# An attention, a dense block and eight experts in one program: a branch laid out the other way, a weight conversion spread over three steps, matmuls regrouped, and one store made conditional

## The chip, the cores and the metric

The kernel runs on one core of a Trainium2 chip. That core has a matrix engine (TensorE, PE in the profile; its weight loads are listed apart as PEld), VectorE (DVE), ScalarE (ACT), GpSimd (POOL) and SyncE (SP). Each engine takes its own list of instructions in order and waits on semaphores for the others. The metric is device time in microseconds (us) of the whole program, smaller being better.

## The reference, cut to what matters

```python
# q, k, v: 2 batches x 8 heads x 768 tokens x 64; a query sees the keys of its own 6-bit bucket
scores = np.where(q_bucket[..., :, None] == k_bucket[..., None, :], q @ k.T / 8, -1e9)
x = (softmax(scores) @ v)                       # as 1536 tokens x 512
h = x @ w_in                                    # 512 -> 2048, weights given as 64-bit floats
g = np.where(h >= 1, h, np.where(h <= -1, 0, (h + 1) ** 2 / 4))
x = g @ w_out                                   # 2048 -> 512
# gate: two experts of 8 for each token, with weights top2_w
for e in range(8):
    for k in range(2):
        mask = top2[:, k] == e
        out[mask] += top2_w[mask, k, None] * (np.maximum(x[mask] @ w1[e], 0) @ w2[e])
```

Which experts a token goes to is known only on the chip, so the size of each expert's work is data.

## The kernel before, in words

The order of all work is written out by hand. There are three stages in a row, with the gate between the last two.

**Attention** (class `Attention`, `run`). There are 96 steps, one for each 128 queries of a head, and four more to drain. Step `t` issues on TensorE the scores of step `t` (L178, L180), the transposes of the probabilities of step `t - 4` (L209), and, from `t = 10` on, one call of `values` (L217): the product of one block of 128 transposed keys with the values of two heads. Six calls fill one PSUM bank. Every sixth step TensorE also computes the bucket bits of a new head (L158). VectorE takes the row minimum of the scores (L189) and some small columns (L191 to L195), ScalarE the exponential (L197) and the copies of the transposes out of PSUM (L210), GpSimd the division by the row sum (L200). The scores have two PSUM buffers: scores `t + 2` wait for the exponential of `t`.

**Dense block** (class `Dense`). 64 pairs (token block c of 384, feature block f of 128) are walked in order. Step `i` issues `hidden` for pair `i` (12 matmuls, L561, into bank `i % 2`) and then `out` for pair `i - 2` (9 matmuls, L584, into three banks). All matrices are split into a high and a low part so that three products make one exact one. `hidden` goes on with ScalarE (L567), VectorE (L570, L573), ScalarE (L574, the high part `gh`) and GpSimd (L575, the low part `gl`). The weights come as 64-bit floats and have to be converted on the chip, one feature block of 1024 columns at a time, in eight steps (`Weights.steps`): an absolute value on ScalarE (L315), a clip (L316) and a shift (L317) on VectorE, four bit combinations of half a block each on VectorE (L311), and a split into high and low part on ScalarE and GpSimd (L307, L308). The first three blocks are converted during the attention, the other 13 in the dense block, one every second step from step 2 on. Before the change all but the split are issued in one step, between the instructions of `hidden`, and the split in the next.

**Experts** (class `Experts`). Nine jobs `j`: the first takes tokens of expert 0 from the first nine token tiles, the second the rest of expert 0, the others one expert each. A job works on a block `o = 0` of up to 384 tokens and, where more came, on further blocks `o = 1, 2, 3`. A block has 11 steps: L720 computes hidden features of step `i`, L714 multiplies those of step `i - 3` by the second matrix; ScalarE and VectorE split the hidden features (L747, L748). Each step exists in up to four widths, chosen by a branch on TensorE alone (L729, L731, L739) from the count of tokens. ScalarE and VectorE also split the weights of the next job (L931, L932). Tokens are gathered by GpSimd (L682), turned by TensorE (L699), and results are scaled by VectorE (L752) and added to the output by GpSimd's scatters (`scatter`, L688, with a small memset L687 ahead of each).

Between two jobs stands `further` (L797): a branch on all five engines that asks whether the job has further blocks. Its one side runs block `o` (11 steps in all widths, and the next `further` inside it); its other side, `over`, stores the rows of the last block, between which stand the first three steps of the next job. Before the change the second side is laid out right behind the branch, and from its end TensorE must jump over the whole first side. The count `more` is read into registers (L843) just ahead of the branch. In the profiled data jobs 0 and 2 have a further block, and the others have none. After job 8 `over` stores all three blocks of 128 rows, whatever the count.

Of the kernel before, what the change touches and what calls it, by code (L numbers as in the profile page):

```python
# [41 lines left out]
NG = TOK // HT  # L42
# [26 lines left out]
class Attention:  # L69
# [175 lines left out]
    def run(self, hooks, drain):  # L245

        lag, nt, plan = 4, self.nt, {}
        for a in range(2):
            for i, j in enumerate((1, 1, 2, 3 + 4 * a, 3, 4)):
                plan.setdefault(j + 4 * a, []).append((self.prep, a, i))  # L250
            plan.setdefault(5 + 6 * a, []).append((self.proj, a, f"x{a}"))
        self.start()
        done = 0
        for t in range(nt + 4):
            pr, j = divmod(t, 12)
            if t < nt:
                self.scores(t)
            if t >= lag:
                self.transposes(t - lag)
            self.soft(t)  # L260
            self.flush(2 if j < 2 else 1)
            if pr < 7:
                for f, a, i in plan.get(j, []):
                    f(2 * pr + 2 + a, i)
            if pr < 8 and j == 0:
                self.load_v(pr)
            if pr < 6 and j in (6, 11):
                self.load(2 * pr + 4 + (j == 11))
            for f in hooks.get(t, []):
                f()  # L270
            if t >= lag + 6:
                self.values(*divmod(t - lag - 6, 6))
                done += 1
            if t >= nt:
                drain(t - nt)
        while done < nt:
            self.values(*divmod(done, 6))
            done += 1
        self.flush()
# [263 lines left out]
class Dense:  # L543
# [8 lines left out]
    def py(self, c):  # L552
        return self.banks[5:8] if c == 1 else self.banks[2:5]

    def hidden(self, i, c, f, extra):
        nc, p, w = self.nc, self.banks[i % 2][:, :HT], self.wt.W[f]
        V, A = nc.vector, nc.scalar
        n = 0
        for k in range(4):
            for a, x in ((0, 0), (0, 1), (1, 0)):  # L560
                nc.tensor.matmul(p, w[:, a, cols(k, 128)], self.X[c][:, x, k], start=n == 0, stop=n == 11)  # L561
                n += 1
        a = self.sb.tile([128, HT], F32, name="ga", bufs=2)
        gh = self.sb.tile([128, HT], F32R, name="gh", bufs=3)
        gl = self.sb.tile([128, HT], F32R, name="gl", bufs=3)
        self.G[c, f] = gh, gl
        A.activation(a, p, AF.Relu, bias=self.half[:, 0:1], scale=0.5)  # L567
        for e in extra[:2]:
            e()
        V.scalar_tensor_tensor(a, a, 1.0, a, op0=ALU.min, op1=ALU.mult)  # L570
        for e in extra[2:3]:
            e()
        V.tensor_tensor(a, p, a, op=ALU.max)  # L573
        A.activation(gh, a, AF.Copy)  # L574
        nc.gpsimd.tensor_sub(gl, a, gh.bitcast(F32))  # L575
        for e in extra[3:]:
            e()

    def out(self, c, f):
        gh, gl = self.G.pop((c, f))  # L580
        w = self.wt.W[f]
        for t in range(3):
            for i, (g, a) in enumerate(((gh, 0), (gh, 1), (gl, 0))):
                self.nc.tensor.matmul(self.py(c)[t], g[:, cols(t, 128)], w[:, a, 512:1024],  # L584
                                      start=f == 0 and i == 0, stop=f == NF - 1 and i == 2)

    def run(self, convert, late, rows):
# [18 lines left out]
        def at(i, f):  # L606
            plan.setdefault(i, []).append(f)

        split = {}
        for i in range(4 * NF + lag):  # L610
            if i < 4 * NF:
                extra = []
                for j in [j for j, s in convert.items() if s == i]:
                    st = wt.steps(j)
                    extra += st[:-1]
                    split.setdefault(i + 1, []).append(st[-1])
                extra += split.get(i, [])
                self.hidden(i, *order[i], extra)
            if i >= lag:
                c, f = order[i - lag]  # L620
                self.out(c, f)
# [16 lines left out]
class Experts:  # L638
# [137 lines left out]
    def over(self, j, o, c):  # L776

        rows = self.rows(j, o)
        if j == NE:
            for f in rows:  # L780
                f()
            return
        if j == 0 and o == 0:
            for i in range(8 + LAG):
                self.tokens(1, 0, i, self.xr)
        for i in range(LAG):
            if i < len(rows):
                rows[i]()
            self.step(j + 1, 0, i, c)
            if j >= 1:  # L790
                self.prefetch(8 * self.expert(j + 1) + 4 + i)

    def further(self, j, o, more, c):

        if self.blocks(j, o) < 1:
            return self.over(j, o - 1, c)
        with self.tc.If(more > o - 1, preferred_fallthrough_block=False) as g:  # L797
            for f in self.rows(j, o - 1):
                f()
            if o > 1:  # L800
# [18 lines left out]
    def job(self, j, c, hooks={}):  # L819

        cn = self.first if j == 0 else self.cn[:, j - 1]
        for i in range(0 if j == 0 else LAG, 8 + LAG):
            self.step(j, 0, i, c)
            if j >= 2 and i == LAG:
# [9 lines left out]
                self.tokens(j + 1, 0, i, self.xr)  # L834
            if j and i == 5:
                self.gather(j, 1, self.xm)
        c = self.load(j + 1, 0) if j < NE else None
        self.further(j, 1, self.number(cn[:, NG:], NG - 1), c)
        return c

    def number(self, cn, most, engines=None):
# [185 lines left out]
```

## Time and profile before

| | us |
|---|---|
| median of 3 runs | 961.88 |
| lowest and highest | 960.09, 964.64 |
| the profiled execution | 965.52 |
| its span, from the first to the last instruction | 963.7 |
| TensorE busy in it | 875.0 |
| VectorE, ScalarE, GpSimd busy | 579.7, 433.1, 393.8 |
| mean granted clock of TensorE | 0.966 |

One execution is profiled; all start times below count from the first instruction of its span. A busy time is the time in which at least one instruction of that engine ran. "Idle before" names the engine or the queue whose signal ended the idle time; "issue" there means that the engine waited for nothing that the profile shows, so that its own list of instructions had not yet delivered one. TensorE's matmuls overlap, so the times of neighbouring rows overlap too. A granted clock of 1 is 2.4 GHz, one of 0.5 is 1.2 GHz.

### The profile page before, as it was taken

Reading aid. Unit: us, or ns where it says so; the run is one execution under the profiler, and the core shown is the slowest. Engines: PE = TensorE matmul, PEld = TensorE weight load, DVE = VectorE, ACT = ScalarE, POOL = GpSimd, SP = SyncE. Lnnn points to the kernel's source line nnn. Section 1 sums busy time; section 2 is a strip of 40 time slices with the busy share of each in tenths; the row PEclk is TensorE's granted clock in tenths of the full one; section 3 lists DMA queues with packets and bytes.
Section 4 is the critical chain, followed back from the end, with each engine's and each line's share of the span. In section 5 each row is a group of like instructions: output and inputs, shape, how many; then the busy total and the mean of one; then the engine's idle time right before and its main releaser. Section 6 shows DMA issues by size and latency. Waiting matters only on the chain.

```text
span 963.7 us, 13751 instructions
## 1 busy us (share of the span) xinstructions
PE 875.0 (91%) x4846; PEld 716.0 (74%) x4846; DVE 579.7 (60%) x1215; ACT 433.1 (45%) x786; POOL 393.8 (41%) x403
## 2 busy tenths in 40 slices
PE   5999999999999898999999999978988968989873
PEld 3666666666687777899899888867877857878763
DVE  7899999988378787532926725326333445354352
ACT  4787787788534434333334432214322334334240
POOL 7777776784244545322221320332123143140332
PEclk8999999999999999999999999979999979999987
DMA  4439212112560000000501421346535376483742
GB/s 148 157 107 265 83 50 83 50 50 94 201 274 1 1 0 1 1 1 1 198 1 63 145 69 36 70 81 159 165 79 134 124 213 167 164 223 101 202 91 37
DMA packets 39883, 98.49 MB, mean 102 GB/s; under 512 B 6080, under 2 KB 15296, under 8 KB 37696
## 3 DMA queue, kind: packets, MB, share of 16 engines
q1 hardware_dynamic: 30688, 73.69, 22.8%
q0 software_dynamic: 8912, 22.50, 11.2%
q8 instruction: 94, 1.54, 0.7%
q14 instruction: 45, 0.37, 0.1%
q10 hardware_dynamic: 144, 0.39, 0.1%
HBM read 80.00 MB, written 16.58 MB: 100 GB/s over the span
## 4 chain that ended last, share of the span: by engine, by line
PE 40%; DMA 33%; DVE 15%; ACT 5%; issue 3%; another core or an unknown queue 2%; POOL 1%; POOLq 0%; SPq 0%; ACTq 0%; DVEq 0%
DMA xr<-xd,idx 16%; DMA out_dram<-yT,il 9%; DMA xm<-xd,idx 8%; PE b L561 7%; PE b L584 7%; PE bank_x L217 6%; PE bank_t L209 5%; PE s L178 4%; DVE TB L311 4%; PE s L180 3%; DVE ga L570 2%; DVE st L189 2%; PE b L714 2%; PE b L720 2%
## 5 line engine op out<-in xcount | busy, mean ns | idle before, releaser
L714 PE MATMUL b<-W,hT 128*128 128x512 f32 x648 | 176.9, 416 | 39.3 <-issue 34.6
L714 PEld LDWEIGHTS b<-W,hT 128*128 128x128 f32 x648 | 122.6, 198 | 65.7 <-issue 41.5
L688 POOL DMA_INDIRECT out_dram<-yT,il x33 | 52.4, 1589 | 258.9 <-DVE yT L752 256.4
L748 DVE SCALAR_TENSOR_TENSOR hT<-b,hT 128x384 fp32r<-128x384 f32 x88 | 49.0, 556 | 178.8 <-ACT hT L747 177.2
L747 ACT ACTIVATE hT<-b 128x384 fp32r<-128x384 f32 x88 | 43.3, 492 | 236.2 <-PE b L720 235.5
L561 PE MATMUL b<-X,W 128*128 128x384 f32 x768 | 147.3, 340 | 0.0
L575 POOL TENSOR_TENSOR gl<-ga,gh 128x384 fp32r<-128x384 f32 x64 | 75.2, 1177 | 165.2 <-ACT gh L574 126.5
L561 PEld LDWEIGHTS b<-X,W 128*128 128x128 f32 x768 | 135.0, 189 | 6.2 <-issue 1.8
L200 POOL TENSOR_SCALAR p<-p,st 128x768 f32<-128x768 f32 x96 | 98.1, 1022 | 63.1 <-DVE st L195 51.4
L584 PE MATMUL b<-W,gh 128*128 128x512 f32 x384 | 120.7, 395 | 0.0
L197 ACT ACTIVATE p<-s,st 128x768 f32<-128x768 f32 x96 | 95.5, 995 | 41.7 <-DVE st L195 34.6
L189 DVE TENSOR_REDUCE st<-s 128x1 f32<-128x768 f32 x96 | 91.7, 955 | 17.7 <-PE s L180 16.1
L720 PEld LDWEIGHTS b<-XT,W 128*128 128x128 f32 x576 | 88.9, 197 | 5.3 <-issue 1.8
L720 PE MATMUL b<-XT,W 128*128 128x256 f32 (+2 forms) x576 | 91.7, 314 | 1.2 <-issue 1.1
L570 DVE SCALAR_TENSOR_TENSOR ga<-ga 128x384 f32<-128x384 f32 x64 | 46.9, 733 | 74.8 <-ACT ga L567 74.8
L932 DVE TENSOR_TENSOR W<-stage,W 128x1024 fp32r<-128x1024 f32 x64 | 78.3, 1224 | 22.0 <-ACT W L931 22.0
L584 PE MATMUL b<-W,gl 128*128 128x512 f32 x192 | 77.6, 404 | 12.8 <-POOL gl L575 12.8
L210 ACT ACTIVATE pT<-bank_t 128x384 f32<-128x384 f32 x192 | 83.4, 488 | 8.9 <-PE bank_t L209 7.9
L217 PE MATMUL bank_x<-pT,vt 128*64 128x384 f32 x384 | 81.8, 510 | 0.4 <-DVE KM L165 0.3
L720 PE MATMUL b<-XA,W 128*128 128x384 f32 (+1 forms) x480 | 81.5, 323 | 0.0
L574 ACT ACTIVATE gh<-ga 128x384 fp32r<-128x384 f32 x64 | 33.6, 525 | 105.9 <-DVE ga L573 105.9
L209 PE MATMUL bank_t<-ident,p 128*128 128x128 f32 x576 | 79.4, 274 | 1.4 <-ACT pT L210 1.4
(171 smaller groups left out, 1303.3 us busy)
## 6 DMA issues: line engine op xcount, KB each, us to landing
stage<-in_w_dram SPq DMA_DIRECT2D x64, 512.0 KB, 4.4
R<-in_wio_dram SPq DMA_DIRECT2D x16, 1024.0 KB, 7.3
raw<-in_qk_dram SPq DMA_DIRECT2D x15, 768.0 KB, 4.3
out_dram<-z SPq DMA_DIRECT2D x15, 256.0 KB, 4.9
vt<-in_vv_dram SPq DMA_DIRECT2D x8, 384.0 KB, 4.8
xd<-TB SPq DMA_DIRECT2D x3, 780.0 KB, 3.7
xd<-z SPq DMA_DIRECT2D x3, 260.0 KB, 6.0
xd<-rows SPq DMA_DIRECT2D x1, 780.0 KB, 6.0
```

What stands on the lines that cost most here:

```text
L189: V.tensor_reduce(st[:, 0:1], s[:, :, :HT], axis=AX.XY, op=ALU.min)
L197: self.A.activation(p.rearrange("p (a b) -> p a b", a=2), s[:, :, :HT], AF.Exp, bias=st[:, 2:3], scale=st[:, 3:4], accum_out=st[:, 5:6])
L200: self.G.tensor_scalar(self.P[t - 1], self.P[t - 1], ps[:, 5:6], 1.0, op0=ALU.mult, op1=ALU.mult)
L209: self.T.transpose(b[:, cols(j, 128)], p[:, cols(3 * g + j, 128)], self.ident)
L210: self.A.activation(self.PT[u, s][:, cols(g, 3), cols(i, 128)], b[:, :HT].rearrange("p (j q) -> p j q", j=3), AF.Copy)
L217: self.T.matmul(xp[cols(s, 64), :HT], self.vt[pr][:, s, kt, :], self.PT[u, s][:, kt, :], start=kt == 0, stop=kt == 5)
L561: nc.tensor.matmul(p, w[:, a, cols(k, 128)], self.X[c][:, x, k], start=n == 0, stop=n == 11)
L575: nc.gpsimd.tensor_sub(gl, a, gh.bitcast(F32))
L584: self.nc.tensor.matmul(self.py(c)[t], g[:, cols(t, 128)], w[:, a, 512:1024], start=f == 0 and i == 0, stop=f == NF - 1 and i == 2)
L714: self.T.matmul(self.banks[2 + b], h[:, a, cols(b, 128)], w2[:, x, 512:1024], start=i == LAG and n == 0, stop=i == LAG + 7 and n == 2)
L720: self.T.matmul(p, w[:, a, cols(k, 128)], X[:, x, k, :N], start=n == 0, stop=n == 11)
L932: nc.vector.tensor_sub(w[:, 1], d, w[:, 0].bitcast(F32))
```

## The change

Four edits. In `run` of the attention `values` is called twice in every second step and not once in each. In `Dense` the eight parts of a block's conversion are placed by a table over the steps s - 1 to s + 2 (s being the step that took seven of them before) and at four places of `hidden`: ahead of L567, behind it, between L570 and L573, and at the end. `out` walks its nine matmuls by operand and then by bank, so that the three that read `gl` come last. In `Experts`, `over` reads the last job's class of size and stores only the first block where the count is at most 128. `further` lays its first side behind the branch, so that `over` is the far side and runs straight on into the next job; the branch gets a label for `o = 1`, and each job places on all five engines, behind its step 6, a hint that this branch will likely be taken. `more` is read at the start of the job.

```diff
@@ Attention.run @@
-            if t >= lag + 6:
-                self.values(*divmod(t - lag - 6, 6))
-                done += 1
+            if t >= lag + 6 and (t - lag) % 2:
+                for _ in range(2):
+                    self.values(*divmod(done, 6))
+                    done += 1
@@ Dense.hidden @@
-    def hidden(self, i, c, f, extra):
+    def hidden(self, i, c, f, early, amid, mid, late):
+        for e in early:
+            e()
         A.activation(a, p, AF.Relu, bias=self.half[:, 0:1], scale=0.5)
-        for e in extra[:2]:
+        for e in amid:
             e()
         V.scalar_tensor_tensor(a, a, 1.0, a, op0=ALU.min, op1=ALU.mult)
-        for e in extra[2:3]:
+        for e in mid:
             e()
         V.tensor_tensor(a, p, a, op=ALU.max)
         A.activation(gh, a, AF.Copy)
         nc.gpsimd.tensor_sub(gl, a, gh.bitcast(F32))
-        for e in extra[3:]:
+        for e in late:
             e()
@@ Dense.out @@
-        for t in range(3):
-            for i, (g, a) in enumerate(((gh, 0), (gh, 1), (gl, 0))):
+        for i, (g, a) in enumerate(((gh, 0), (gh, 1), (gl, 0))):
+            for t in range(3):
@@ Dense.run @@
-        split = {}
+        conv = {}
+        for j, s in convert.items():
+            for n, (d, place) in enumerate([(-1, 1), (0, 2), (1, 3), (2, 0), (2, 0), (2, 0), (2, 0), (2, 1)]):
+                conv.setdefault(s + d, ([], [], [], []))[place].append(lambda j=j, n=n: wt.steps(j)[n]())
-                extra = []
-                for j in [j for j, s in convert.items() if s == i]:
-                    st = wt.steps(j)
-                    extra += st[:-1]
-                    split.setdefault(i + 1, []).append(st[-1])
-                extra += split.get(i, [])
-                self.hidden(i, *order[i], extra)
+                self.hidden(i, *order[i], *conv.get(i, ([], [], [], [])))
@@ Experts.over @@
         if j == NE:
-            for f in rows:
-                f()
+            n = self.number(self.cn[:, j - 1, o:o + 1], len(CLASSES) - 1)
+            with self.tc.If(n > 0) as g:
+                for f in rows:
+                    f()
+            with g.Else():
+                rows[0]()
             return
@@ Experts.further @@
-        with self.tc.If(more > o - 1, preferred_fallthrough_block=False) as g:
+        kw = {"label": f"further{j}"} if o == 1 else {}
+        with self.tc.If(more > o - 1, preferred_fallthrough_block=True, **kw) as g:
@@ Experts.job @@
+        more = self.number(cn[:, NG:], NG - 1)
...
+            if i == 6:
+                self.tc.mark_branch_hint_location(f"further{j}", "LikelyTaken", engines=list(mybir.ALL_ENGINES))
         c = self.load(j + 1, 0) if j < NE else None
-        self.further(j, 1, self.number(cn[:, NG:], NG - 1), c)
+        self.further(j, 1, more, c)
```

## Rows read from the trace of the kernel before

**Rows 1.** Busy us (count) of PE, PEld, DVE, ACT, POOL by stretch; clock, DMA, GB/s.
```profile
160.70:190.30 29.60, 29.60 (x186) 18.72 (x184) 28.39 (x64) 23.27 (x50) 21.45 (x23) 1.00 0.20 67
264.00:392.00 128.00, 116.18 (x570) 101.28 (x569) 98.65 (x131) 52.74 (x80) 64.34 (x38) 1.00 0.14 56
611.00:948.00 337.00, 295.34 (x1592) 262.70 (x1591) 147.14 (x223) 106.37 (x160) 89.92 (x100) 0.93 0.53 139
```

**Rows 2.** Timeline of TensorE, attention: start, us, line, operation, count.
```profile
25.11 0.62 PE L178 MATMUL s<-KS,QH 128*128 128x384 f32 x2
26.58 0.61 PE L178 MATMUL s<-KS,QH 128*128 128x384 f32 x2
...
41.43 0.61 PE L178 MATMUL s<-KS,QH 128*128 128x384 f32 x2
43.77 0.61 PE L178 MATMUL s<-KS,QH 128*128 128x384 f32 x2
...
258.96 4.74 PE L217 MATMUL bank_x<-pT,vt 128*64 128x384 f32 x28
```

**Rows 3.** Waits of 264 to 392 us: total us, times, longest.
```profile
PE b L584 <- POOL gl L575: 11.8, 11, 1.1
```

**Rows 4.** Timeline of two steps of the conversion, VectorE and GpSimd.
```profile
295.84 1.05 DVE L316 TENSOR_SCALAR TB<-TB 128x1024 f32<-128x1024 f32 x1 [2.08 <-ACT TB L315]
296.81 1.34 DVE L570 SCALAR_TENSOR_TENSOR ga<-ga 128x384 f32<-128x384 f32 x1
298.08 0.68 DVE L317 TENSOR_SCALAR TB<-TB 128x1024 int32<-128x1024 int32 x1
298.68 0.54 DVE L573 TENSOR_TENSOR ga<-b,ga 128x384 f32<-128x384 f32 x1
299.15 3.30 DVE L311 SCALAR_TENSOR_TENSOR TB<-R,TB 128x512 int32<-128x512 int32 x4
302.37 0.54 DVE L570 SCALAR_TENSOR_TENSOR ga<-ga 128x384 f32<-128x384 f32 x1
...
293.93 2.41 POOL L308 TENSOR_TENSOR W<-TB,W 128x1024 fp32r<-128x1024 f32 x1 [2.38 <-ACT W L307]
296.30 1.44 POOL L575 TENSOR_TENSOR gl<-ga,gh 128x384 fp32r<-128x384 f32 x1
303.69 2.40 POOL L308 TENSOR_TENSOR W<-TB,W 128x1024 fp32r<-128x1024 f32 x1 [2.39 <-ACT W L307]
```

**Rows 5.** Branches by line and engine: count, ns minimum/median/maximum, first and last start.
```profile
L797 PEldq COMPARE_BRANCH  x20: 67/1840/5479, 600.2 to 949.2; - x20
...
L797 ACTq COMPARE_BRANCH  x20: 34/38/55, 601.5 to 947.4; - x20
L797 DVEq COMPARE_BRANCH  x20: 43/47/72, 602.2 to 948.9; - x20
...
L731 PEldq COMPARE_BRANCH  x80: 65/176/4332, 659.6 to 912.2; - x80
```

**Rows 6.** TensorE's waits, 760 to 948 us (jobs 3 to 8): total us, times, longest.
```profile
PE b L714 <- issue: 26.4, 6, 9.0
```

**Rows 7.** Timeline of TensorE where one job passes into the next.
```profile
671.56 3.50 PE L714 MATMUL b<-W,hT 128*128 128x512 f32 x9 [3.59 <-DVE W L932]
...
739.33 3.14 PE L714 MATMUL b<-W,hT 128*128 128x512 f32 x9 [2.57 <-issue]
...
815.26 3.85 PE L714 MATMUL b<-W,hT 128*128 128x512 f32 x9 [3.90 <-issue]
...
821.09 2.23 PE L714 MATMUL b<-W,hT 128*128 128x512 f32 x9
```

**Rows 8.** Timeline of the end: a step of job 8, first and last scatter.
```profile
940.26 0.86 PE L714 MATMUL b<-W,hT 128*128 128x512 f32 x3
...
949.94 1.62 POOL L688 DMA_INDIRECT out_dram<-yT,il  x1 [12.79 <-DVE yT L752]
...
954.36 1.59 POOL L688 DMA_INDIRECT out_dram<-yT,il  x1 [0.87 <-issue]
```

## Prediction, made before the changed kernel ran

> **What bounds it now.** I read the busy times by stretch first. TensorE is busy all the time in the attention (29.60 of 29.60 us for twelve steps), and less in the stretch with the conversions (116.18 of 128.00) and in the experts (295.34 of 337.00, at a mean granted clock of 0.93) [rows 1]. So TensorE's own list sets the pace everywhere; it can be shortened in the first stretch, and its holes filled in the other two. The timelines and waits then say who ends each hole. In the conversion stretch it is GpSimd's `gl` alone, 11.8 us in eleven waits [rows 3]. In the experts the holes lie where one job passes into the next and end by "issue": TensorE's own list had nothing to give [rows 6, 7]. The branch rows say why: the same branch L797 costs 67 ns where it falls through and up to 5479 ns where it jumps, on TensorE alone; on ScalarE and VectorE it never costs over 72 ns [rows 5].
>
> **Attention.** A step without `values` takes 26.58 - 25.11 = 1.47 us on TensorE, one with it 43.77 - 41.43 = 2.34; so a lone call costs 0.87. At the end seven calls run back to back in 4.74 us, 0.68 each [rows 2]. Two steps cost 4.68 now, and 1.47 + 2.34 + 0.68 = 4.49 with both calls together: 0.19 less, and 45 such pairs make 8.6. That is one end. The other is VectorE, which is busy 28.39 us of the 29.60 that twelve steps take [rows 1]; 1.2 are free there, against 6 x 0.19 = 1.1 that TensorE gives back, and it would have to run without a gap. Steps now come alternately early and late, and scores `t + 2` wait for the exponential of `t`, behind VectorE's minimum. A loss is not excluded if that wait opens. I take 6 us off, two thirds of the bound, since the heavy stretches will be VectorE's and the light ones TensorE's; the ends are 9 off and 2 on.
>
> **Conversion.** Two steps hold one block. From one L316 to the next of its kind is a loop: ScalarE's L315, then L316, L570, L317, L573, the four L311, L570 again; VectorE stands idle 2.08 us in each round, waiting for L315 [rows 4]. L308 recurs every 303.69 - 293.93 = 9.76 us [rows 4]. After the change L315 and L317 are done a step ahead of need, and the L311 stand where VectorE waited for TensorE; the 2.08 goes. What is late next is VectorE with GpSimd. L570 takes 0.54 alone and 1.34 with `gl` running beside it [rows 4]: it waits until GpSimd is through. VectorE's round is then 3.30 + 1.05 + 0.68 + 2 x 0.54 + 2 x 0.54 = 7.2, and between the first L573 and the second L570 the data must still pass through two of the three ScalarE instructions behind which the 2.08 arises (L574, L567 and L315, which is gone): about half of it, 1.0. That is 8.2, and one more clash of 0.8 with L308 (2.41) or `gl` makes 9.0. Without clashes the 11.8 us of waits [rows 3] go wholly; with two or three the round stays near 9.76 and nothing goes. At 9.0 it is 0.76 shorter, over eleven rounds 8 us. I take 7, since some rounds will clash twice; ends 0 and 12. The reordered `out`, which asks for `gl` after six matmuls and not two, helps only these same waits. A block's split is now issued one step later; its first reader stands two steps behind, so this hides until the round is late by as much.
>
> **The far branch.** Jobs 3 to 7 lose 26.4 us to "issue" in six waits [rows 6], job 1 loses 3.59 (the row names L932, but L797 held the queue until then) [rows 7]: 30 us at six passages. Each also lowers the clock: behind job 4's passage nine L714 take 3.85 us, where nine take 2.23 a little later [rows 7], 1.6 more; six times that is an estimate of 10. Total 40. After the change these jobs jump at the branch, hinted five steps ahead, and `over` runs on without a jump. The trace has no hinted branch. Bounds: 67 ns, the fall-through, and 5479 ns, the far jump [rows 5]. I take 0.2 us, near the 176 ns median of L731 [rows 5], the nearest row of jumps whose target is held. What remains is the code behind the target: L731 too has a jump of 4332 ns [rows 5], so a jump into code not yet there stalls again. Three L720 steps stand at the head of `over` to cover it. I leave 2 us per passage, the middle between nothing and job 4's 3.90 [rows 7], and so take 40 - 12 = 28 off. Jobs 0 and 2 go the other way: they fall through, but inside they jump far without a hint and jump once more over `over`. One added far jump costs about what job 2's lone one does now, 2.57 us [rows 7]; without half of it covered, 1.5 each, so 3 back. Net 25 off; ends 3 on (hint without effect) and 37 off. The nine hints on five engines and the earlier read of `more` lie beside TensorE's queue: nothing, and if that cover is gone some tenths of a us per job.
>
> The Trainium skill speaks against this part (Runtime: NRT & Kernel Launch, section Instruction fetch mechanics): it says that prefetch is purely sequential and that a taken branch out of the fetched window must first fetch its target. The trace agrees for the branches it has, 67 ns against 5479 [rows 5]; no run here shows a hint. By the page alone the term would be 3 on and not 25 off.
>
> **The last store.** The three last scatters start at 949.94 and 954.36, 4.42 us from the first to the third [rows 8]. Job 8's steps have three L714 each [rows 8], one row block and so the lowest class: its count is at most 128 and one scatter stays. The added read and branch come while GpSimd waits 12.79 us for VectorE [rows 8] and cost nothing; if that cover failed, some 0.4 us. I take 4.4 off, ends 3 and 5.
>
> **Sum.** 6 + 7 + 25 + 4.4 = 42.4. The profiled execution took 965.5, so 923.1; it lies 3.6 above the median of the runs, which makes 961.9 - 42.4 = 919.5.
>
> **Rivals.** (a) *The hint has no effect*, so the far stall only moves from the end of `over` to the branch. For it: a taken branch here always paid when far, and the page named above states it as a rule. Against it: nothing in the trace, which has no hint. Then 961.9 - 6 - 7 - 4.4 + 3 = 947.5. (b) *VectorE takes over* in the attention and in the conversion: its 28.39 of 29.60 [rows 1] and the clash of L570 [rows 4] speak for it, the 2.08 us of idle time against it. Then 961.9 - 25 - 4.4 = 932.5. (c) *Slower:* the hinted target displaces the code in use on ScalarE or VectorE, which have no far jump at L797 now [rows 5]. Place: between step 6 and the end of each job. Price: a far fetch, some 4.4 us in eight jobs, 35 us, while TensorE gets nothing: 947.5 + 35 = 982.5. It decides the sign from 14 / 8 = 1.8 us per job. Against it: those engines hold few instructions per job.
>
> **Numbers.** Forecast 0.52, (a) 0.25, (b) 0.17, (c) 0.05; 0.01 is left. The forecast's own range is 905 to 931 (terms at 9, 11, 32 and 5 off, and at 2, 2, 23 and 4 off). The range of 8 in 10 is 904 to 949: it takes in (b) and about half of (a). About 0.5%, 4.8 us, is what a measurement can tell from no change. Slower by more is (c), 0.05; within it lies the upper edge of (a), 0.06; faster has 0.89.
>
> **What would show it.** Right: L797 on TensorE has no row over 1 us at the end of jobs 1 and 3 to 7, and the "issue" waits of 760 to 948 us fall from 26.4 to about 10; L308 recurs every 9.0 us and `gl` ends hardly any wait of TensorE; pairs of attention steps take 4.5 to 4.6 us; one scatter after the last matmul. Wrong: a far L797 of 3 to 5 us now at the branch itself (a); scores waiting for the exponential, or L308 still every 9.7 us (b); gaps on ScalarE or VectorE behind step 6 (c).

## The result, and the profile after

The changed kernel takes 931.02 us (median of four runs, 928.71 to 932.29), the kernel before 961.82 beside it (four runs, 960.09 to 964.64): a ratio of 0.9674, 95% interval 0.9642 to 0.9707, or 31 us less. Run once more beside other kernels it stood at 0.9629 (0.9606 to 0.9651), 36 us less. I had forecast 919.5 with a range of 904 to 949: the sign and the range hold, and the gain is three quarters of the 42.4 I had summed. That is closer than the reasons were, and in part luck: of the four terms one was nothing, one was nearly twice as large, one was half as large, and the largest came about in another way than I said. These errors cancel in part.

The profiled execution took 928.71 us with a span of 926.9. Most lines have moved: L308 is L309 here, L311 is L312, L316 and L317 are L317 and L318, L567 is L570, L570 and L573 are L573 and L576, L575 is L578, L688 is L689, L714 is L715, L720 is L721, L729 and L731 are L730 and L732, L752 is L753, L797 is L803. I read it in the order of the prediction. First the busy times by stretch, with the columns of [rows 1]; the last stretch begins 37 us earlier here, so that it ends as long ahead of the program's end. The stage has become shorter, so the same 337 us hold 1726 of TensorE's instructions where they held 1592.

```profile
160.70:190.30 29.60, 28.55 (x185) 19.09 (x185) 27.70 (x64) 23.00 (x51) 21.52 (x23) 1.00 0.19 67
264.00:392.00 128.00, 127.93 (x634) 111.98 (x631) 101.46 (x137) 57.66 (x84) 64.84 (x42) 1.00 0.14 56
574.00:911.00 337.00, 311.23 (x1726) 276.75 (x1726) 159.10 (x267) 110.48 (x168) 98.87 (x106) 0.97 0.54 143
```

Beside [rows 1] the three stretches went three ways. In the attention TensorE *lost* its full list: 28.55 of 29.60, with nearly the same count of instructions (185, before 186), where it was busy throughout before. In the conversion it has no hole left (127.93 of 128.00, before 116.18). In the experts it is busy 15.9 us more of the 337, at a granted clock of 0.97 after 0.93.

**Attention.** TensorE's waits from 35 to 240 us: total us, times, longest. Before, the first two had 1.0 in two waits and 0.3 in one.

```profile
PE s L178 <- ACT p L197: 4.6, 10, 1.1
PE bank_x L158 <- DVE X L222: 3.5, 6, 0.6
```

The scores wait for the exponential, as the prediction named it for the case where VectorE takes over, and L158, the first matmul of the next head, waits for L222, VectorE's eviction of the `values` just finished. VectorE's timeline shows what stands in front of that L222:

```profile
170.22 0.96 DVE L143 SCALAR_TENSOR_TENSOR QM<-raw,QH 64x768 fp32r<-64x768 f32 x1
171.21 0.96 DVE L189 TENSOR_REDUCE st<-s 128x1 f32<-128x768 f32 x1
172.19 0.15 DVE L191 TENSOR_SCALAR st<-st 128x1 f32<-128x1 f32 x1
172.27 0.78 DVE L193 SCALAR_TENSOR_TENSOR st<-st 128x2 f32<-128x2 f32 x1
172.97 0.15 DVE L195 RECIPROCAL st<-st 128x1 f32<-128x1 f32 x1
173.05 0.53 DVE L222 TENSOR_TENSOR X<-bank_x,X 128x384 fp32r<-128x384 f32 x1
```

From 170.22 to 173.58 these six follow each other without a gap, and L158 starts at 173.64. From the first scores to the last it is 234.89 us now, 235.66 before; then the attention's last calls take 17.39 us between the first and the third step of the dense layers where they took 14.41. (Of these 3.0 us, 1.7 belong to one drop of the clock in this one execution, a mean of 0.67 from 260 to 264 us, where the last `values` calls take 7.07 us; in experiment 4, at a clock of 1.00, they take 5.38. The other profiles with the same pairs have 15.69 or 15.70.) From the first scores to the third dense step it is 255.63 us, before 253.72; five other profiles with the same pairs and all of VectorE's work have 254.2 to 255.3, and five without pairs, that of before among them, 253.6 to 254.2. The term is no gain but a loss of some tenths to 1.5 us.

**Conversion.** No wait of TensorE is left from 264 to 392 us, where `gl` had 11.8 in eleven [rows 3]. VectorE and GpSimd in one round, to be held against [rows 4]:

```profile
290.05 1.09 DVE L573 SCALAR_TENSOR_TENSOR ga<-ga 128x384 f32<-128x384 f32 x1 [1.35 <-ACT ga L570]
291.18 0.56 DVE L576 TENSOR_TENSOR ga<-b,ga 128x384 f32<-128x384 f32 x1
291.65 0.93 DVE L318 TENSOR_SCALAR TB<-TB 128x1024 int32<-128x1024 int32 x1
292.61 3.22 DVE L312 SCALAR_TENSOR_TENSOR TB<-R,TB 128x512 int32<-128x512 int32 x4
295.75 0.55 DVE L573 SCALAR_TENSOR_TENSOR ga<-ga 128x384 f32<-128x384 f32 x1
296.22 0.68 DVE L317 TENSOR_SCALAR TB<-TB 128x1024 f32<-128x1024 f32 x1
296.82 0.54 DVE L576 TENSOR_TENSOR ga<-b,ga 128x384 f32<-128x384 f32 x1
298.43 1.40 DVE L573 SCALAR_TENSOR_TENSOR ga<-ga 128x384 f32<-128x384 f32 x1 [1.06 <-ACT ga L570]
...
288.33 2.39 POOL L309 TENSOR_TENSOR W<-TB,W 128x1024 fp32r<-128x1024 f32 x1 [3.53 <-ACT W L308]
290.69 1.34 POOL L578 TENSOR_TENSOR gl<-ga,gh 128x384 fp32r<-128x384 f32 x1
292.46 1.01 POOL L578 TENSOR_TENSOR gl<-ga,gh 128x384 fp32r<-128x384 f32 x1 [0.44 <-POOL gl L578]
297.00 2.41 POOL L309 TENSOR_TENSOR W<-TB,W 128x1024 fp32r<-128x1024 f32 x1 [3.52 <-ACT W L308]
```

L309 recurs every 297.00 - 288.33 = 8.67 us (before 9.76). VectorE's wait of 2.08 for the bias step is gone; what remains is 1.1 to 1.4 us for ScalarE's L570 (L567 before) and one slow L573 (1.09 to 1.40, alone 0.55) in each round, the one clash that I had counted. Both end before TensorE asks: the stage is bound by TensorE's own list now.

**The far branch.** The rows of L803 from 640 to 900 us, beside [rows 5]:

```profile
L803 PEldq COMPARE_BRANCH  x9: 65/3653/4702, 646.6 to 889.1; - x9
L803 ACTq COMPARE_BRANCH  x9: 38/45/50, 647.8 to 890.1; - x9
```

The hint was to bring TensorE's jump down to some 0.2 us, and it did not. At the six usual joints it takes 3.59, 4.13, 3.40, 4.36, 4.33 and 4.70 us, 4.08 in the mean; at the end of `over` it was 4.82 in the mean. Yet the waits at the joints fell. TensorE's largest waits from 723 to 911 us (the jobs of [rows 6]), then one passage as TensorE's timeline, with the row of its branch:

```profile
PE b L721 <- issue: 12.2, 6, 4.2
```

```profile
813.79 0.60 PE L700 MATMUL b<-ident,xr 128*128 128x128 f32 x4
814.15 2.34 PE L715 MATMUL b<-W,hT 128*128 128x512 f32 x9
816.33 0.60 PE L700 MATMUL b<-ident,xr 128*128 128x128 f32 x4
816.68 2.35 PE L715 MATMUL b<-W,hT 128*128 128x512 f32 x9
820.61 3.71 PE L721 MATMUL b<-XA,W 128*128 128x384 f32 x20 [1.58 <-issue]
...
L803 PEldq COMPARE_BRANCH  x1: 4359/4359/4359, 815.8 to 815.8; - x1
```

The branch starts at 815.83 and holds TensorE's queue for 4.36 us, to 820.2. But when it starts, the engine still has 3.20 us of matmuls in hand (to 819.03), and the next one starts at 820.61, so it idles 1.58. 26.4 us of "issue" [rows 6] have become 12.2.

**The end.** GpSimd's one scatter that is left:

```profile
915.47 1.62 POOL L689 DMA_INDIRECT out_dram<-yT,il  x1 [5.61 <-DVE yT L753]
```

From here to the end of the span it is 11.46 us; from the first scatter before it was 13.79 [rows 8]. The two scatters that are gone spanned 4.42, and 2.3 of that came out.

### The profile page after: what moved, and what is told of

The parts are those of the page before. It is cut to its first block, busy times and chain, and to the rows that moved or that the text cites. A ratio compares the mean times of both kernels' runs of the same rounds, so it can differ in the third digit from the quotient of the medians.

```text
span 926.9 us, 13769 instructions
## 1 busy us (share of the span) xinstructions
PE 859.8 (93%) x4846; PEld 712.8 (77%) x4846; DVE 574.3 (62%) x1213; ACT 433.7 (47%) x786; POOL 387.6 (42%) x399
## 4 chain that ended last, share of the span: by engine, by line
PE 49%; DMA 26%; DVE 15%; ACT 3%; another core or an unknown queue 3%; issue 2%; POOL 0%; SPq 0%; POOLq 0%; ACTq 0%; DVEq 0%
PE b L562 13%; PE b L587 12%; DMA xr<-xd,idx 11%; DMA xm<-xd,idx 9%; PE b L721 5%; DMA out_dram<-yT,il 5%; DVE st L189 5%; PE bank_x L217 4%; PE b L715 4%; PE bank_t L209 3%; PE s L178 3%; PE s L180 2%; ACT p L197 2%; DVE st L193 2%
## 5 line engine op out<-in xcount | busy, mean ns | idle before, releaser
L715 PE MATMUL b<-W,hT 128*128 128x512 f32 x648 | 168.0, 399 | 3.4 <-ACT hT L748 1.8
L689 POOL DMA_INDIRECT out_dram<-yT,il x31 | 49.2, 1586 | 236.4 <-DVE yT L753 235.3
L715 PEld LDWEIGHTS b<-W,hT 128*128 128x128 f32 x648 | 116.8, 188 | 27.0 <-DVE yT L753 2.6
L578 POOL TENSOR_TENSOR gl<-ga,gh 128x384 fp32r<-128x384 f32 x64 | 69.6, 1088 | 145.5 <-ACT gh L577 121.8
L573 DVE SCALAR_TENSOR_TENSOR ga<-ga 128x384 f32<-128x384 f32 x64 | 46.1, 720 | 91.0 <-ACT ga L570 91.0
L721 PE MATMUL b<-XT,W 128*128 128x256 f32 (+2 forms) x576 | 92.3, 314 | 10.0 <-issue 10.0
L721 PEld LDWEIGHTS b<-XT,W 128*128 128x128 f32 x576 | 88.5, 198 | 15.1 <-issue 12.5
L587 PE MATMUL b<-W,gh 128*128 128x512 f32 x384 | 99.8, 395 | 0.0
L721 PE MATMUL b<-XA,W 128*128 128x384 f32 (+1 forms) x480 | 82.4, 326 | 9.8 <-issue 9.4
L721 PEld LDWEIGHTS b<-XA,W 128*128 128x128 f32 x480 | 78.1, 199 | 14.3 <-issue 11.0
L587 PEld LDWEIGHTS b<-W,gh 128*128 128x128 f32 x384 | 71.2, 188 | 11.5
L209 PEld LDWEIGHTS bank_t<-ident,p 128*128 128x128 f32 x576 | 68.0, 142 | 9.4 <-issue 4.1
```

The source lines that it names most:

```text
L209: self.T.transpose(b[:, cols(j, 128)], p[:, cols(3 * g + j, 128)], self.ident)
L689: d = self.G.indirect_dma_start(out=self.dst[:, :], out_offset=bass.IndirectOffsetOnAxis(ap=ix, axis=0), in_=y, in_offset=None, compute_op ...
L715: self.T.matmul(self.banks[2 + b], h[:, a, cols(b, 128)], w2[:, x, 512:1024], start=i == LAG and n == 0, stop=i == LAG + 7 and n == 2)
L721: self.T.matmul(p, w[:, a, cols(k, 128)], X[:, x, k, :N], start=n == 0, stop=n == 11)
```

## The experiments

The four parts touch different stages, so most experiments take one part alone, from the kernel before or out of the kernel after. Times on different chips differ by some us; each ratio is to the kernel before, run beside it.

**1. The hint left out of the changed kernel.**

```diff
-            if i == 6:
-                self.tc.mark_branch_hint_location(f"further{j}", "LikelyTaken", engines=list(mybir.ALL_ENGINES))
```

> The changed kernel without the nine hints; the new layout of the branch, the early read of the count and all else stay. Theory A (the hint does nothing: in the changed kernel L803 still takes 3.4 to 4.7 us at the branch of jobs 1 and 3 to 7, so the gain in the experts comes from the layout alone): the time stays at 931 within 0.5%, and these six rows stay at 3.4 to 5.5 us. Theory B (the hint starts the fetch early and so shortens each far branch, from 5.0 us on average before to 4.1): the six rows grow by about 1 us each, and the time by 4 to 8 us.

928.98 us, ratio 0.9625 (0.9587 to 0.9664): as fast as with the hint, theory A. The rows of its branch from 640 to 900 us, its waits from 555 to 950 (in the changed kernel L721 has 19.5 in eleven there), and then the changed kernel's hints on TensorE:

```profile
L803 PEldq COMPARE_BRANCH  x9: 65/3979/4503, 643.1 to 888.2; - x9
...
PE b L721 <- issue: 16.9, 12, 2.4
PE b L715 <- issue: 2.8, 4, 2.0
```

```profile
L1032 PEldq BRANCH_PREFETCH_HINT  x9: 31/31/45, 0.8 to 1.6; - x9
```

The six usual jumps take 4.14 us in the mean without a hint, 4.08 with it. The Trainium skill (Runtime: NRT & Kernel Launch, section Instruction fetch mechanics) says that a taken branch out of the fetched window must first fetch its target; these rows agree: 4.08 us with the hint, 4.14 without, and 65 ns where the branch falls through. The hint does nothing for the jumps here that these runs can show. But its row says more: all nine hint instructions run in the first 1.7 us of the program, and so they do on the other four engines; none runs behind a step 6, hundreds of us later. Whether such an instruction names a place further on, no row tells. So these runs show that the hint as it came out is worth nothing, not that one executed five steps ahead of its branch would be. It has a small price: the first scores start at 10.26 to 10.54 us in the five profiles with the hints and at 9.84 to 10.15 in the nine without.

**2. The hint marked three steps later.** It might have stood too early, its target fetched and lost again before the branch.

```diff
-            if i == 6:
+            if i == 9:
```

> The changed kernel with its hint behind step 9 and not step 6, so that fewer branches and less code lie between the hint and its branch. Theory A (the hint starts no fetch here): L803 stays at 3.4 to 5.5 us at the branch of jobs 1 and 3 to 7, and the time at that of the changed kernel within 0.5%. Theory B (the hint fetches, and what it fetched is displaced by the code of steps 7 to 10): these rows fall below 3 us and the time by 4 us or more.

932.19 us, ratio 0.9649 (0.963 to 0.9668). The row of its branch, same stretch, and of its hints:

```profile
L803 PEldq COMPARE_BRANCH  x9: 65/4114/4726, 646.0 to 892.8; - x9
...
L1032 PEldq BRANCH_PREFETCH_HINT  x9: 31/31/45, 0.8 to 1.6; - x9
```

4.26 us in the mean of the six, as theory A has it. But the hint instructions run when they did with the mark behind step 6, in the first 1.7 us. So the edit did not move what it was to move, as far as the trace shows, and whether a hint can stand too early stays open.

**3. The branch alone, put into the kernel before:** the other side falls through, the label, the hint and the earlier read.

```diff
-        with self.tc.If(more > o - 1, preferred_fallthrough_block=False) as g:
+        kw = {"label": f"further{j}"} if o == 1 else {}
+        with self.tc.If(more > o - 1, preferred_fallthrough_block=True, **kw) as g:
...
+        more = self.number(cn[:, NG:], NG - 1)
...
+            if i == 6:
+                self.tc.mark_branch_hint_location(f"further{j}", "LikelyTaken", engines=list(mybir.ALL_ENGINES))
```

> The kernel before with the branch part alone (layout, label, hint, early read of the count). Theory A (the branch part alone makes the 24 us that the experts' stretch lost): 936 to 940 us, and a stretch of 360 to 364 us from the first to the last expert matmul. Theory B (a part of the 24 comes with the earlier start of the experts, against the weights' transfers): more than 942 us.

945.28 us, ratio 0.9793 (0.9765 to 0.982): 20 us off. The time is that of theory B, but its reason did not show: the experts' stretch is 364.8 us here, with the late start, and 362.4 to 368.4 with the earlier one; the 24 us of theory A rest on two single profiles (more on that below). With experiment 1 the gain is the layout's, not the hint's; the earlier read of `more` goes along in both and was not tried apart. How the layout does it can be read at the six usual joints of three kernels (from TensorE's timeline and the starts and lengths of the long branches; means, in us):

| kernel | far branch | matmuls still in hand when it starts | idle at the joint |
|---|---|---|---|
| before | 4.82 | 1.87 | 4.92 |
| changed | 4.08 | 2.95 | 2.08 |
| changed, no hint | 4.14 | 2.94 | 1.69 |

Three things add up to the 17.0 us that six joints gain (29.5 less 12.5). The jump is 0.7 shorter. It starts with 1.1 more of matmuls in hand: ahead of it stand nine-matmul L715 steps, and at the end of `over` stood L720 steps. That this is the reason was not tried, nor why the jump is shorter. Six times 1.8 is 10.9; the other 6.1 lie behind the jump. Before, the joint at 925.9 (6.32 us idle) had a second far jump, L729 with 3.39, in the code just reached, and that at 772.4 (9.02 us) lost 5.8 us between a weight load at 777.11 and its matmul at 782.93, for which the trace names no cause. After, one joint with a second jump is left (4.25 us idle): L803 at 748.74 and, in the code reached, an L730 of 3.06 us at 752.93. Over the whole program, TensorE's branches of more than 0.5 us sum to 75.2 us before, 53.7 in the changed kernel (59.8 in its second profile), 52.2 without hint and 55.8 with the branch alone. Why some jumps in the expert code are short and others long wasn't tried. That joint has the second stall in six of the eight profiles of the new layout (4.25 to 6.58 us idle), two of them without a hint (4.47 and 4.45), and not in the other two, with the branch alone and in experiment 1 (1.53 and 1.43); so it isn't the hint's, and the gap between 2.08 and 1.69 in the table is this one joint.

What a single profile says of this stage must be read with care. From the first matmul of the experts to the end of the last one, the six profiled kernels with the old layout took 379.6 to 386.4 us (mean 383.5) and eight with the new one 362.4 to 368.4 (mean 365.3), although inside each set the experts' code is the same but for the hints and the last store. The kernel before's profile was at the slow end of its set, the changed kernel's at the fast end: 24.0 us between these two, 18.2 between the means, 13.6 of it idle time and 4.6 busy time, at a granted clock of 0.94 to 0.96 in the old layout and 0.96 to 0.99 in the new one.

**4. The paired values alone, put into the kernel before.**

```diff
-            if t >= lag + 6:
-                self.values(*divmod(t - lag - 6, 6))
-                done += 1
+            if t >= lag + 6 and (t - lag) % 2:
+                for _ in range(2):
+                    self.values(*divmod(done, 6))
+                    done += 1
```

> The kernel before with the attention's values of two steps together, nothing else. Theory A (what TensorE saves is lost to waits for the exponential and, in the drain, for the transposes' copies: from the first scores to the third dense step it took 253.7 us before and 255.6 after): 962 to 965 us, no gain or a loss of up to 3 us. Theory B (the pairing gains its 6 us and another edit, the conversion's early ScalarE work, spoils the drain): 955 to 957 us.

963.85 us, ratio 0.999 (0.9973 to 1.0007): nothing clear of noise, theory A. TensorE's timeline of scores and of the next head's L158, one start per step:

```profile
169.56 0.62 PE L178 MATMUL s<-KS,QH 128*128 128x384 f32 x2
171.50 0.62 PE L178 MATMUL s<-KS,QH 128*128 128x384 f32 x2 [0.32 <-ACT p L197]
173.79 0.84 PE L158 MATMUL bank_x<-raw,pp 64*18 64x384 f32 x8 [0.59 <-DVE X L222]
176.00 0.62 PE L178 MATMUL s<-KS,QH 128*128 128x384 f32 x2
177.38 0.59 PE L178 MATMUL s<-KS,QH 128*128 128x384 f32 x2
180.34 0.62 PE L178 MATMUL s<-KS,QH 128*128 128x384 f32 x2
```

A plain pair takes 180.34 - 176.00 = 4.34 us, 0.35 less than the 4.69 before. The pair with L158 takes 176.00 - 169.56 = 6.44, where it took 5.46. Twelve steps hold one such heavy pair, a second pair with L158 that takes 5.62, and four plain ones. The plain pairs gain about what the heavy ones lose: the pairing works on TensorE, and gives it back within the same twelve steps.

**5 and 6. Less work for VectorE, with single and with paired values.** Both leave out L143 from head 4 on, so two instructions of 0.96 us in twelve steps. The paired one differs from the single one by the edit of experiment 4.

```diff
+            if h > 3:
+                return
             self.V.scalar_tensor_tensor(QM[64:128], q[64:128], -0.125, QH[64:128].bitcast(F32), op0=ALU.mult, op1=ALU.subtract)
```

> The kernel before, with VectorE's L143 (the low half of the queries, 0.96 us each) left out from head 4 on, so the scores of those heads lack their low part. It takes work from VectorE alone, two instructions in twelve steps of attention. TensorE as the bound of the attention: no change, 0 to -1 us against before, and pairs of steps stay at 4.69 us. VectorE as the bound already before: about -15 us, two times 0.96 in each of the eight sets of twelve steps, and pairs shorter in the heavy sets.

> The kernel before with the values of two steps together and the same L143 left out from head 4 on. If VectorE's load is what eats the gain of the paired order (a), the pairs with L158, 6.45 us with that load, fall by half a us or more, and the attention comes out at least 2 us below that of the lone L143 experiment. If it is the delay from a step's scores over minimum and exponential (b), which the shorter list of VectorE doesn't shorten, plain pairs stay at 4.35, those with L158 at 6.3 to 6.5, and both kernels agree within 1 us.

Single: 964.24 us, ratio 0.9979 (0.9952 to 1.0005). Paired: 958.14, ratio 0.9917 (0.9889 to 0.9944). Waits of TensorE in the paired one from 35 to 240 us, then the last scores of the single one and of the paired one (the first start at 9.89 in both; L178 is L180 here):

```profile
PE s L180 <- ACT p L199: 4.3, 9, 1.0
PE bank_t L211 <- ACT pT L212: 0.6, 2, 0.3
```

```profile
245.31 0.61 PE L180 MATMUL s<-KS,QH 128*128 128x384 f32 x2
```

```profile
239.94 0.60 PE L180 MATMUL s<-KS,QH 128*128 128x384 f32 x2
```

With single values VectorE's relief is worth nothing clear of noise: the attention was TensorE's. With paired values the scores' stretch is 5.4 us shorter: the wait of L158 for L222 (3.6 in six in experiment 4) is gone from the list, and both pairs with L158 take 5.6 to 5.8. The waits for the exponential stay at 4.3, so they are not what cost the gain. Theory (a) holds: it is VectorE's list. Of the 5.4 us, 1.0 is lost again where the attention ends (15.70 instead of 14.41 us between the first and the third dense step, 3.35 instead of 3.66 from the last scores to the first dense step), as in experiment 4.

**7. The pairs in the other steps.** Would the heavy pair fare better if the pairs fell on even steps (and without the hint)?

```diff
-            if t >= lag + 6 and (t - lag) % 2:
+            if t >= lag + 6 and (t - lag) % 2 == 0:
```

> The changed kernel without hints and with the two calls of values in the even steps of the attention and not in the odd ones, which are also the steps that hold the bucket bits L158. Theory A (the pairing gains 0.34 us in a plain pair of steps, 4.35 for 4.69, and loses 1 us in the pair with L158, 6.45 for 5.46, because that L158 stands in the long step and its bank is read out late): the pair with L158 comes to 5.1 to 5.5 us, the attention loses 4 to 9 us against the kernel without hints, 920 to 925 us where that one is at 929. Theory B (VectorE's own load limits all pairs, wherever L158 stands): the same time as without hints within 2 us.

930.93 us, ratio 0.9629 (0.9611 to 0.9646), beside 930.84 for the changed kernel. L158 waits for L222 no more, but the scores wait 5.7 us for the exponential and L217 1.5 for L165; the scores span 238.04 us, 2.4 more than in the kernel before, of which the attention's end gives back 1.0 (13.39 instead of 14.41). Theory A is out, and the time is that of B: the parity only moves the loss.

**8 and 9. The changed kernel again, and without hint and pairs.** Number 8 is the changed kernel as it is; number 9 takes out the edits of experiments 1 and 4.

> The changed kernel once more, for a comparison with the three kernels beside it. Both theories: 0.962 to 0.969 of the kernel before, as it stood against it the first time (0.9674).

> The changed kernel without hints and with one call of values in each step, as before the change. Theory A (the pairing as made gains nothing): within 0.3% of the changed kernel without hints. Theory B (the pairing loses in the drain what it does not win): 1 to 3 us faster than that.

930.84 us, ratio 0.9629 (0.9606 to 0.9651), and 928.5 us, ratio 0.9613 (0.9593 to 0.9633). The hint and the pairs can be left out without loss. The simpler kernel has the lower median, but the intervals overlap: it is not shown to be faster.

**10. The conversion alone, put into the kernel before:** the table of eight splits and the order of `out`.

```diff
+        conv = {}
+        for j, s in convert.items():
+            for n, (d, place) in enumerate([(-1, 1), (0, 2), (1, 3), (2, 0), (2, 0), (2, 0), (2, 0), (2, 1)]):
+                conv.setdefault(s + d, ([], [], [], []))[place].append(lambda j=j, n=n: wt.steps(j)[n]())
...
-                self.hidden(i, *order[i], extra)
+                self.hidden(i, *order[i], *conv.get(i, ([], [], [], [])))
```

> The kernel before with the conversion's table and the new order of the out matmuls alone. Theory A (the waits for gl go and nothing takes their place): 947 to 950 us, 12 to 15 us off, a round of 8.4 to 8.7 us from one L309 to the next. Theory B (the conversion's gain in the changed kernel rests on the attention's later end): under 8 us off.

952.33 us, ratio 0.9867 (0.9838 to 0.9896): 12.8 us off beside 965.2 for the kernel before, so theory A by the difference. In its profile the 26 steps from the third on take 110.94 us, in that of before 123.68: 12.7.

**11. Only the order of `out`, put into the kernel before.**

```diff
-        for t in range(3):
-            for i, (g, a) in enumerate(((gh, 0), (gh, 1), (gl, 0))):
+        for i, (g, a) in enumerate(((gh, 0), (gh, 1), (gl, 0))):
+            for t in range(3):
```

> The kernel before with the order of the matmuls in out alone, so gl is asked for behind six and not two. If the order hides GpSimd's lateness by itself (a), the waits for gl (11.8 us) fall below 3 and the time falls by 8 to 12 us. If the table of splits does the work (b), the round stays at 9.76 us and each wait is only moved: 0 to -3 us. I give (b) 0.6.

964.12 us, ratio 0.998 (0.9955 to 1.0005). TensorE's waits from 264 to 392 us, and GpSimd in the same kernel:

```profile
PE b L561 <- DVE ga L573: 5.7, 11, 0.5
PE b L584 <- POOL gl L575: 2.5, 10, 0.3
```

```profile
284.83 2.40 POOL L308 TENSOR_TENSOR W<-TB,W 128x1024 fp32r<-128x1024 f32 x1 [2.38 <-ACT W L307]
...
294.60 2.40 POOL L308 TENSOR_TENSOR W<-TB,W 128x1024 fp32r<-128x1024 f32 x1 [2.38 <-ACT W L307]
```

The waits for `gl` fall from 11.8 to 2.5 as (a) said, but a new one opens at L561 (5.7), the round stays at 294.60 - 284.83 = 9.77 us, and the 26 steps take 123.64, as before: (b). The waits sum to 8.2 instead of 11.8 and not a tenth of a us comes out: the 3.6 us are counted as busy time of TensorE now (119.82 in the stretch, before 116.18, for the same 570 instructions). VectorE still waits 2.09 us for L315 in each round; the round sets the pace, and TensorE meets it at one place or another. The table is what shortens the round. Whether it needs the new order wasn't tried.

**12. The changed kernel with its last job as before:** three scatters.

```diff
-            n = self.number(self.cn[:, j - 1, o:o + 1], len(CLASSES) - 1)
-            with self.tc.If(n > 0) as g:
-                for f in rows:
-                    f()
-            with g.Else():
-                rows[0]()
+            for f in rows:
+                f()
```

> The changed kernel without the comparison for the last job, so three scatters again behind the last matmul. By the trace of the change (last matmul to end 15.2 us before, 12.9 after) it is 2.3 us slower than the changed kernel; by the prediction's own term 4.4; if the end of the program waits for something else, 0.

933.5 us, ratio 0.9668 (0.9634 to 0.9703). Its interval takes in 0.9674 of the changed kernel and overlaps with that of 0.9629, so the time can't tell 2.3 us from 0. Its trace can: from its first scatter, at 917.03, to the end of the span it is 13.61 us, where the changed kernel takes 11.46. This is 2.1 us, near the forecast of 2.3 and not the prediction's 4.4. Where the rest goes can be seen in GpSimd's own rows at the end, first the changed kernel's, then this one's. A DRAIN is the long instruction with which its list ends:

```profile
L782 POOLq INC_SWDGE_SEM  x1: 1850/1850/1850, 915.3 to 915.3; - x1
...
L803 POOLq INC_SWDGE_SEM  x1: 1844/1844/1844, 917.4 to 917.4; - x1
...
L1032 POOLq DRAIN  x3: 46/109/6849, 919.2 to 926.7; - x3
```

```profile
L1028 POOLq INC_SWDGE_SEM  x2: 1101/1128/1154, 916.8 to 918.7; - x2
...
L799 POOLq INC_SWDGE_SEM  x1: 1173/1173/1173, 921.4 to 921.4; - x1
...
L1028 POOLq DRAIN  x3: 46/115/7177, 922.6 to 930.4; - x3
```

Here each of the three scatters has an INC_SWDGE_SEM beside it, 3.43 us in sum, and the DRAIN starts 1.17 us behind the start of the last scatter (921.44). In the changed kernel one stands beside the scatter, a second of 1.84 us behind it with no scatter at its side, 3.69 in sum, and the DRAIN starts 3.77 us behind the scatter's start. So 2.6 of the 4.4 are lost there, and 0.3 come back because the DRAIN and what follows are shorter. What the second one is for, and whether the conditional brings it, isn't shown.

## Why the prediction was right, and where its steps failed

The time falls within the range because TensorE's list bounds the kernel, and two of the holes I had read in it (`gl` in the conversion, "issue" at the joints) were filled. By single parts the gains are 1.0 (experiment 4), 20 (3), 12.8 (10) and 2.1 (12), together 36 of the 42.4 forecast, and 31 and 36 in the two measurements of the whole. The 1.0 is not clear of noise. That the sum lies so near is luck in part: the attention and the far branch gave each some 5 us less than forecast and the last store 2 less, but the conversion 6 more.

- **Attention: 6 off, measured 0 to 1, and in the traces a loss of some tenths to 1.5 us.** The bound of TensorE was sound: 0.19 per pair foreseen, 0.35 seen in plain pairs. The step that failed is "1.2 are free there, against 6 x 0.19": I took the free time of VectorE as if it lay anywhere in the twelve steps. It is wanted around the steps with L158, and there six instructions run without a gap. This is rival (b) for this stretch, shown by experiments 4 to 6: with 1.92 us less on VectorE, 5.4 come out of the scores' stretch, nearly the 6 I had taken. It isn't the one wait for L222: experiment 7 takes that away and gains nothing. I had also left out the end of the attention, which costs 1.0 more with pairs.
- **Conversion: 7 off, measured 12.8.** The mechanism held: L315 and L317 a step early, the 2.08 us gone, one clash left per round. The round was mis-sized: 9.0 forecast, 8.67 measured, and it is TensorE's own length now. So was the count: from the first L308 of the dense block to the last there are twelve rounds, not eleven, and twelve times 1.09 make 13. The 1.0 that I left for ScalarE's instructions is there (1.06 to 1.35), but with two L573 clashes I would have stopped at 9.76; one clash and the wait fit beside TensorE. 12 was my upper end. The order of `out` is worth nothing by itself (11).
- **Far branch: 25 off, measured 20 alone and 18 between the means of the profiles.** The size is near, the reason is wrong. "I take 0.2 us" for the hinted jump failed: 4.08 us, 4.14 without a hint (1), 4.26 with the later mark (2). So did "hinted five steps ahead": the hints run in the first 1.7 us of the program. By rival (a) the term should then have been 3 on. That failed too, and at the same step: I took a far jump to cost the same wherever it stands. It costs TensorE its length less the matmuls in hand (and 0.3 to 0.7 until the next one starts), and at the head of the branch there are 1.1 us more of these than at the end of `over` (3). The clock's part, an estimate of 10, stands against 4.6 that the busy time fell. The 3 us for jobs 0 and 2 didn't show: job 2 idles 0.86 and 2.57 us at its two jumps before, and 1.01 and 1.67 in the second profile of the changed kernel.
- **Last store: 4.4 off, measured 2.1 to 2.3.** One scatter stays, as read from job 8's steps. "The added read and branch cost nothing" holds for the branch (45 ns on GpSimd). The step that failed is that the 4.42 between the scatters come off whole: I did not ask what GpSimd does between its last scatter and its end. That takes 2.6 us more now (12), 1.84 of it in an INC_SWDGE_SEM with no scatter beside it.
- **Rival (c)** had no trace: that line's branch costs ScalarE at most 63 ns and VectorE 81 in the changed kernel. Since the hints ran at the program's start, this case can't show what one inside a job would displace.

Of the signs named ahead, "no L797 over 1 us" and "L308 every 9.0 us, `gl` ends hardly a wait" were the ones that told: the first came out wrong at once, though the "issue" waits fell to 12.2 where I had said about 10; the second came out right. Of the signs against, both the far L797 at the branch (a) and the scores' waits for the exponential (b) were there.

## What to carry to other kernels

A far jump cost TensorE here its length less the matmuls that its queue had already handed over, so ask at which place most are in hand, and look at the second jump in the code that it reaches. Before judging a hint, look up when its instruction runs. Where an engine is nearly full beside the bounding one, don't compare free time with need over a stretch: look for the instructions whose deadline moves (here L222 and the scores' chain, around a deferred `values`), and take work off that engine to see whether it is the bound. And when a wait is moved by a new order of the matmuls, read the round of the slower engine: if it stays, so does the time.

## What was not expected of the hardware

A hint marked behind step 6 or step 9 became an instruction in the first 1.7 us of the program, on all five engines, and did not change the length of TensorE's far jump (4.08 and 4.26 us, 4.14 without). GpSimd runs an INC_SWDGE_SEM of up to 1.85 us beside its indirect DMAs; behind the shortened last store one of 1.84 us stands alone, and it takes back part of what the two scatters had cost. And the same expert code, with other code ahead of it, took 379.6 to 386.4 us from kernel to kernel, more than two of the four parts of this change are worth; which addresses make a jump far wasn't settled.
